# Two steps of a first chunk: exponents in a second PSUM bank and weight pieces taken in twos, in a Fourier-mixing and hard-swish kernel

## The chip, the cores and the metric

The kernel runs on one core of one Trainium2 chip. The metric is the time of one execution on the device in microseconds (us); lower is better.

## What is computed

The reference mixes a tensor with a two-dimensional Fourier transform, keeps the real part, and sends every row through a two-layer network with a hard-swish gate. `x` and the output are float32, the two weight matrices float64.

```python
x: (8, 3008, 256)      w_in: (256, 2048)      w_out: (2048, 256)
X = np.fft.fft(np.fft.fft(x, axis=1), axis=2).real      # (24064, 256) as rows
h = X @ w_in
g = h * np.clip(h + 3.0, 0.0, 6.0) / 6.0
out = g @ w_out                                         # (24064, 256)
```

## The kernel before

**The main work.** The eight batches are four pairs (`Pair`). The sequence transform of a pair is made in two stages (`stage1`, `stage2`); the transform along the 256 columns is folded into `w_in` (`fold_w_in`), so that its result lies in the SBUF tile `W1` (and one column of it in `WN`). A pair has 24 chunks, and a chunk eight steps, one for each two of the sixteen blocks of 128 hidden units. A step of a chunk is `mlp1` (four matmuls on TensorE into the PSUM tiles `u` and `v`, line 337, then two additions, two scaled relus on ScalarE, L379, and two gates on VectorE, L382, that leave the tile `a`), and `mlp2` (seven matmuls, L422, over seven combinations of blocks of `w_out`, kept in `G`). Only the first chunk of all uses the plain form `mlp2_first` (four matmuls of 512 columns, L406, "acc" below), since the combined blocks of `G` aren't ready. All matmuls on float32 show as two passes in the records, so four matmuls are "x8".

**The weights.** Both weight matrices come in as 64-bit words, in sixteen pieces of 128 x 512 (512 KB each), and are turned into float32 by hand, from the two 32-bit halves of each word. Pieces 0 to 3, 8, 9, 10 and 11 belong to `w_in`, the others to `w_out`. For a piece `j`:

- `exponent_a(j)`, here a(j): two ScalarE instructions (L532) that put exponent bytes into a tile `PM`, of which there are two, used in turn;
- `mantissa(j)`, here m(j): two VectorE instructions (L553, L554);
- `exponent_b(j)`, here ex(j): two fp16 matmuls on TensorE (L542) that gather the exponents in a PSUM tile; for pieces 5 and 15 it is one VectorE subtraction instead;
- `exponent_c(j)`, here c(j): one ScalarE instruction (L545) in place in PSUM;
- `join(j)`: VectorE multiplies mantissa and exponent into a tile `wi` (`w_in`, L562, one instruction) or into `G` (`w_out`, L568, two).

`head(j)` is a(j), m(j) and, for some pieces, the load of a later one (`load_w`, a DMA on GpSimd's queue, POOL). `tail(j)` is c(j) and the join. `unit(j)` is ex(j), then `head(j + 1)`, then `tail(j)`. When two pieces of `w_in` are joined, `fold_w_in(n, h)` multiplies them with the cosine table on TensorE (tile `spare`, L591; with h = 0 also the small matmuls `pw`, L599), and a postponed copy (`copy_all`) takes the product to `W1` and `WN` on ScalarE (L603, L605). With h = 1 the `WN` part goes out as four small DMAs on SyncE's queue, SP (L608).

**The order.** Nothing is scheduled by a planner (`manual_schedule`): every engine executes its instructions in the order in which the Python code emits them. In the first chunk the weights are converted between the steps. `DUE` says which units follow which step; `fourth_step` writes the fourth step's order out by hand. So the third step (s = 2) is `mlp1` of step 4 (here mlp1(3), counting from 0), acc(2), `unit(8)`, `unit(9)`; the fourth (s = 3) is acc(3), fold(1,0), units 10 and 11, ex(12), fold(3,0), ex(13), mlp1(4), fold(1,1), fold(3,1). SyncE's queue meanwhile holds, in this order, the late part of the stage-1 result (`zd<-z`, L833), stage-2 tables (`T`, L614), the four `WN` DMAs of this step, then more of `zd` and `T` and, in the sixth step, the load `g<-zd` (L268) that `stage2` needs in the eighth.

**PSUM.** There are eight banks: four of pool `ps_a`, three of `ps_h` (tag "uv": `u`, `v` and `pw` take them in turn) and one of `ps_d`. While `starting` holds, exponents go to `ps_h`; afterwards `bank` gives them the single bank of `ps_d`. So ex(j + 1) must wait there until join(j) has read the bank.

Of the kernel before, what the change touches and what calls it, by code (L numbers as in the profile page):

```python
# [7 lines left out]
F32 = mybir.dt.float32  # L8
I32 = mybir.dt.int32
U32 = mybir.dt.uint32  # L10
I16 = mybir.dt.int16
U8 = mybir.dt.uint8
F16 = mybir.dt.float16
# [45 lines left out]
def kernel(  # L59
# [11 lines left out]
    P = nc.NUM_PARTITIONS  # L71
# [29 lines left out]
    ps_h = ctx.enter_context(tc.tile_pool(name="ps_h", bufs=3, space=PSUM))  # L101
# [90 lines left out]
    starting = [True]  # L192

    def bank(shape, name):
        if starting[0]:
            return ps_a.tile(shape, F32, tag="acc", name=name)
        return ps_d.tile(shape, F32, tag="d", name=name)
# [129 lines left out]
    def mlp1(ch, fc):  # L327
        gr, of, nq = ch.ck // 2, ch.ck % 2 * TB, ch.nq
        q, qn = ch.pr.q[gr], ch.pr.qn[gr]
        u = ps_h.tile([P, 2, TB], F32, tag="uv", name="u")  # L330
        v = ps_h.tile([P, 2, TB], F32, tag="uv", name="v")
        for blk, ps in ((0, u), (1, v)):

            r = slice(0, P - blk)
            for i in range(2):
                f = fc + i * NF
                nc.tensor.matmul(ps[:, i, 0:nq], W1[r, blk, f * P:(f + 1) * P], q[r, blk, of:of + nq],  # L337
                                 start=True, stop=True)
        s = spool.tile([P, 2, TB], F32, tag="s", name="s")
        for i in range(2):  # L340
            f = fc + i * NF
            nc.vector.scalar_tensor_tensor(s[:, i, 0:nq], qn[:, of:of + nq], WN[:, f:f + 1], u[:, i, 0:nq],  # L342
                                           op0=AL.mult, op1=AL.add)


        a = apool.tile([P, 2, 2, TB], F32, tag="a", name="a")
        t = spool.tile([P, 2, 2, TB], F32, tag="t", name="t")
        ch.a[fc] = a
        if ch.last:
            activate_last(a, t, s, u, v, nq)  # L350
            return
        nc.vector.tensor_tensor(u[:], s[:], v[:], op=AL.add)  # L352
        relu(t[:, 0], u[:], 1.0 / 6.0)
        nc.vector.tensor_tensor(v[:], v[:], s[:], op=AL.subtract)  # L354
        relu(t[:, 1], v[:], -1.0 / 6.0)
        gate(a[:, 0], t[:, 0], u[:])
        rev, tk, vk = (m.rearrange("p i (k n) -> p (i k) n", n=N2) for m in (a[:, 1], t[:, 1], v[:]))
        gate(rev[:, :, ::-1], tk, vk)
# [19 lines left out]
    def relu(t, h, scale):  # L378
        nc.scalar.activation(t, h, AF.Relu, bias=half[:], scale=scale)  # L379

    def gate(dst, t, h):
        nc.vector.scalar_tensor_tensor(dst, t, 1.0, h, op0=AL.min, op1=AL.mult)  # L382
# [17 lines left out]
    def mlp2_first(ch, fc):  # L400
        a = ch.a.pop(fc)
        for h in range(2):
            if fc == 0:
                ch.acc[h] = ps_a.tile([P, 2, TB], F32, tag="acc", name="acc")
            for f in range(2):
                nc.tensor.matmul(ch.acc[h][:], G[:, (B11, B12, B21, B22)[2 * f + h], fc, :], a[:, :, f],  # L406
                                 start=(fc == 0 and f == 0), stop=(fc == NF - 1 and f == 1))
        if fc == NF - 1:
            ch.r = epool.tile([P, 2, 2, TB], F32, tag="r", name="r")
            for h in range(2):  # L410
                for m in range(2):
                    nc.scalar.mul(ch.r[:, m, h], ch.acc[h][:, m], (1 - 2 * m) / WS)
# [59 lines left out]
    def store(ch, m):  # L472
        o = epool.tile([P, TB // DH, 2, DH], F32, tag="o", name="o")
        for h in range(2):
            turn(ch, o, m, h)
        send(ch, o, m)
# [15 lines left out]
    wpool = wctx.__enter__()  # L492
# [4 lines left out]
    WB = 512  # L497
# [3 lines left out]
    raw, difs, exs, fracs, w = {}, {}, {}, {}, {}  # L501
# [26 lines left out]
    def exponent_a(j):  # L528
        top = raw[j][:].bitcast(I16).rearrange("p (n four) -> p n four", four=4)[:, :, 3]
        for i in range(2):  # L530
            low = PM[j % 2][:, i].bitcast(U8).rearrange("p (n two) -> p n two", two=2)[:, :, 0]
            nc.scalar.activation(low, top, AF.Identity, bias=bias[:, i:i + 1], scale=(1 - 2 * i) / 16.0)  # L532

    def exponent_b(j):
        pm = [PM[j % 2][:, i].bitcast(F16) for i in range(2)]
        if j in (5, len(PIECES) - 1):
            exs[j] = wpool.tile([P, WB], F32, tag="ex", bufs=2, name="ex")
            nc.vector.tensor_tensor(exs[j][:], pm[0], pm[1], op=AL.subtract)
            return
        exs[j] = ps_h.tile([P, WB], F32, tag="uv", name="ex") if starting[0] else bank([P, WB], "ex")  # L540
        for i in range(2):
            nc.tensor.matmul(exs[j][:], E[:, i], pm[i], start=(i == 0), stop=(i == 1))  # L542

    def exponent_c(j):
        nc.scalar.activation(exs[j][:].bitcast(I32), exs[j][:], AF.Identity, scale=2.0 ** 23)  # L545

    def mantissa(j):
        st = raw.pop(j)
        hi = st[:].rearrange("p (n two) -> p n two", two=2)[:, :, 1]
        lo = st[:].bitcast(U32).rearrange("p (n two) -> p n two", two=2)[:, :, 0]  # L550
        top = wpool.tile([P, WB], I32, tag="top", bufs=3, name="top")
        frac = top[:].bitcast(F32)
        nc.vector.tensor_scalar(top[:], hi, 0xFFFFF, 0x100000, op0=AL.bitwise_and, op1=AL.bitwise_or)  # L553
        nc.vector.scalar_tensor_tensor(frac, lo, 2.0 ** -32, top[:], op0=AL.mult, op1=AL.add)  # L554
        fracs[j] = frac
# [79 lines left out]
    nc.sync.dma_start(out=CE[:], in_=dim[:, :, D:])  # L635
    E = wpool.tile([P, 2, P], F16, tag="E", name="E")
    nc.scalar.copy(E[:], CE[:])
    PM = [wpool.tile([P, 2, WB], I16, tag="PM", bufs=2, name="PM") for j in range(2)]
    for pm in PM:
        nc.vector.memset(pm[:].rearrange("p i n -> p (i n)").bitcast(I32), 0x64006400)  # L640
    for b in range(2):
# [7 lines left out]

    def head(j):  # L650
        exponent_a(j)
        mantissa(j)
        if j in NEXT:
            load_w(NEXT[j])

    def tail(j):
        exponent_c(j)
        join(j)

    def unit(j):  # L660
        exponent_b(j)
        if j + 1 < len(PIECES):
            head(j + 1)
        tail(j)

    def fold_now(n, *hs):
        for h in hs:
            fold_w_in(n, h)

    def copy_all():  # L670
        while copies:
            copies.pop(0)()


    def see(x):
        nc.gpsimd.tensor_copy(seen[:], x)
# [28 lines left out]

    head(0)
    exponent_b(0)
    keep_awake(1)
    head(1)
# [71 lines left out]
    def chunk(s):  # L781
        p, ck, fc = steps[s]
        return chunks[p][ck], fc


    DUE = [(6,), (7,), (8, 9), (), (14,), (15,), (), ()]
    head(4)
    mlp1(*chunk(0))
    exponent_b(4)
# [5 lines left out]
    unit(5)  # L795


    def fourth_step():
        mlp2_first(*chunk(3))
        fold_now(1, 0)  # L800
        unit(10)
        copy_all()
        unit(11)
        exponent_b(12)
        fold_now(NWI // 2 + 1, 0)
        head(13)
        tail(12)
        copy_all()
        exponent_b(13)
        tail(13)  # L810
        mlp1(*chunk(4))
        fold_now(1, 1)
        fold_now(NWI // 2 + 1, 1)
        head(14)
        copy_all()

    prev = None
    for s, (p, ck, fc) in enumerate(steps):
        if ck == 0 and fc == 0:
            at = beside(p)  # L820
        for f, a in at.get(ck * NF + fc, ()):
            f(*a)
        if s < NF:

            if s == 3:
                fourth_step()
            else:
                mlp1(*chunk(s + 1))
                if s == NF - 1:
                    combine(*chunk(NF))  # L830
                mlp2_first(*chunk(s))
            for dst, src in later[2 * s:2 * s + 2]:
                nc.sync.dma_start(out=dst, in_=src)  # L833
            for j in DUE[s]:
                unit(j)

            if s == 5:
                see(chunk(s + 1)[0].a[s + 1][:, 0, 0, 0:1])
                mix_w_out(0)
                mix_w_out(1)  # L840
            if s == NF - 1:
                mlp1(*chunk(NF + 1))
        else:
            if s + AHEAD < len(steps):
                mlp1(*chunk(s + AHEAD))
            if s + 1 < len(steps):
                combine(*chunk(s + 1))
            if s < NF + 2:
                mix_w_out(s - NF + 2)
            if prev and fc < 3:  # L850
                if fc > 0:
                    store(prev, fc - 1)
                elif not prev.first:
                    finish(prev)
            mlp2(*chunk(s))
        if fc == NF - 1:
            prev = chunks[p][ck]
# [81 lines left out]
```

## Time and profile before

| | |
|---|---|
| median of 3 runs | 1976.12 us (1975.09 to 1976.62) |
| span of the profiled execution | 1975.1 us |
| TensorE busy, share of the span | 99% |
| VectorE, GpSimd, ScalarE busy | 73%, 71%, 35% |
| chain that ended last | TensorE 93%, VectorE 3%, others 1% or less |
| TensorE clock in fortieths of the span | full, but for 0.9 in the first and 0.8 in the second |

One fortieth of the span is 49.4 us, so the second one covers 49.4 to 98.8 us, where the first chunk's steps lie. A line of the timeline holds start, duration, engine, source line, operation, tiles, and in brackets how long the engine was idle before it and who ended that. A line of the chain holds start, duration, engine and tile. [...]two exponent matmuls show 0.59 us and the next instruction can start 0.43 us after them.

### The profile page before, as it was taken

The page shows a single profiled execution, that of the slowest core. Times are in us where ns is not written, and L with a number is a line of the kernel's source. Part 1 is how long each engine was busy: PE and PEld are TensorE (multiplying, and loading weights), DVE is VectorE, ACT ScalarE, POOL GpSimd, SP SyncE. Part 2 cuts the span into 40 slices and gives each one's busy share as a digit, 9 for nine tenths or more (in the row PEclk, how much of TensorE's full clock was granted, in tenths as well). Part 3 has the DMA queues.
Part 4 walks back from the last instruction along what each step waited for, and adds up shares of the span by engine and source line. Part 5 has one row for each costly group of instructions (what it writes and reads, how often), then busy time and mean ns, then how long its engine had stood idle before and what let it go on. Part 6 is the DMA issues. An engine that isn't in the chain of part 4 may idle for free.

```text
span 1975.1 us, 27615 instructions
## 1 busy us (share of the span) xinstructions
PE 1945.8 (99%) x9134; PEld 1674.1 (85%) x9134; DVE 1437.4 (73%) x2776; ACT 686.9 (35%) x1167; POOL 1399.9 (71%) x1593
## 2 busy tenths in 40 slices
PE   8899999999999999999999999999999999999998
PEld 4578888888998888888898888888889888888887
DVE  6687767677787676776777777777678777777776
ACT  5533333333333333333333333333333333333332
POOL 3068778786787787777668877778667667666765
PEclk9899999999999999999999999999999999999999
DMA  8421121211112121220111221212110101111000
GB/s 229 159 68 52 51 57 50 54 48 35 27 36 51 41 51 52 56 52 24 38 31 30 66 58 43 51 41 55 36 25 21 29 16 23 27 23 27 18 21 20
DMA packets 144701, 93.34 MB, mean 47 GB/s; under 512 B 116743, under 2 KB 130059, under 8 KB 144558
## 3 DMA queue, kind: packets, MB, share of 16 engines
q1 hardware_dynamic: 134294, 57.89, 12.0%
q0 software_dynamic: 9472, 33.49, 6.0%
q8 instruction: 72, 1.18, 0.3%
q14 instruction: 71, 0.58, 0.1%
q10 hardware_dynamic: 792, 0.20, 0.0%
HBM read 54.22 MB, written 37.32 MB: 46 GB/s over the span
## 4 chain that ended last, share of the span: by engine, by line
PE 93%; DVE 3%; ACT 1%; DMA 1%; issue 1%; SPq 0%; DVEq 0%; POOL 0%; ACTq 0%
PE acc L422 55%; PE v L337 16%; PE u L337 16%; PE ps L213 2%; PE ps L286 2%; DVE a L382 1%; PE acc L406 1%; DMA xt<-in_x_dram,IX 1%; DVE s L342 1%; ACT t L379 1%; PE spare L591 0%; DVE o L480 0%; DVE u L363 0%; ACT PM L532 0%; DMA T<-in_c_stage_dram 0%
## 5 line engine op out<-in xcount | busy, mean ns | idle before, releaser
L396 POOL TENSOR_TENSOR c<-a 128x512 f32<-128x512 f32 (+1 forms) x375 | 468.8, 1250 | 398.9 <-PE acc L422 353.6
L422 PE MATMUL acc<-c,G 128*128 128x256 f32 (+1 forms) x3008 | 696.9, 374 | 0.0
L379 ACT ACTIVATE t<-u,half 128x512 f32<-128x512 f32 (+1 forms) x384 | 260.7, 679 | 1102.6 <-DVE u L352 1023.1
L422 PEld LDWEIGHTS acc<-c,G 128*128 128x128 f32 x3008 | 565.4, 190 | 71.1
L342 DVE SCALAR_TENSOR_TENSOR s<-qn,WN,u 128x256 f32<-128x256 f32 (+1 forms) x768 | 330.1, 471 | 352.2 <-PE u L337 351.6
L422 PE MATMUL acc<-a,G 128*128 128x256 f32 (+1 forms) x2256 | 538.8, 374 | 0.0
L422 PEld LDWEIGHTS acc<-a,G 128*128 128x128 f32 x2256 | 423.4, 190 | 54.9
L337 PE MATMUL v<-q,W 127*128 127x256 f32 (+1 forms) x1536 | 389.4, 375 | 2.3 <-DVE a L382 2.3
L337 PE MATMUL u<-q,W 128*128 128x256 f32 (+1 forms) x1536 | 388.8, 375 | 0.0
L382 DVE SCALAR_TENSOR_TENSOR a<-t,u 128x512 f32<-128x512 f32 (+2 forms) x448 | 263.8, 600 | 102.7 <-ACT t L379 99.1
L337 PEld LDWEIGHTS u<-q,W 128*128 128x128 f32 x1536 | 286.5, 190 | 56.6 <-issue 15.8
L337 PEld LDWEIGHTS v<-q,W 127*128 127x128 f32 x1536 | 288.6, 190 | 42.5 <-DVE a L382 1.9
L396 POOL TENSOR_TENSOR c<-a,c 128x256 f32<-128x256 f32 (+1 forms) x375 | 268.9, 717 | 29.4
L396 POOL TENSOR_TENSOR c<-c,a 128x256 f32<-128x256 f32 (+1 forms) x375 | 268.6, 716 | 29.4
L352 DVE TENSOR_TENSOR u<-s,v 128x512 f32<-128x512 f32 x352 | 245.0, 696 | 38.3 <-DVE s L342 1.8
L382 DVE SCALAR_TENSOR_TENSOR a<-t,v 128x512 f32<-128x512 f32 (+1 forms) x480 | 263.4, 565 | 0.3 <-ACT t L379 0.2
L379 ACT ACTIVATE t<-v,half 128x512 f32<-128x512 f32 (+1 forms) x384 | 260.6, 679 | 0.4 <-issue 0.2
L354 DVE TENSOR_TENSOR v<-v,s 128x512 f32<-128x512 f32 x352 | 243.7, 692 | 0.0
L396 POOL TENSOR_TENSOR r<-w,e 128x256 f32<-128x256 f32 (+1 forms) x92 | 88.8, 987 | 3.6
L430 ACT ACTIVATE e<-acc 128x512 f32<-128x512 f32 (+2 forms) x186 | 84.5, 545 | 3.4 <-PE acc L422 3.3
L480 DVE STREAM_TRANSPOSE o<-r 128x256 f32<-128x256 f32 (+1 forms) x192 | 72.5, 415 | 0.2
L213 PE MATMUL ps<-y,F 94*96 94x512 f32 x120 | 61.3, 601 | 5.2 <-ACT q L289 5.2
(97 smaller groups left out, 798.0 us busy)
## 6 DMA issues: line engine op xcount, KB each, us to landing
out_dram<-o SPq DMA_DIRECT2D x746, 32.0 KB
zd<-z SPq DMA_DIRECT2D x24, 384.0 KB
g<-zd SPq DMA_DIRECT2D x36, 256.0 KB
xt<-in_x_dram POOLq DMA_DIRECT2D x21, 384.0 KB, 4.3
qn<-qd SPq DMA_DIRECT2D x19, 256.0 KB
st<-in_moe_w_in_dram POOLq DMA_DIRECT2D x8, 512.0 KB, 8.3
st<-in_moe_w_out_dram POOLq DMA_DIRECT2D x8, 512.0 KB, 5.7
g<-zd SPq DMA_DIRECT2D x12, 257.0 KB
```

The lines of the kernel that those rows point to most:

```text
L213: nc.tensor.matmul(ps[0:PZ], F[0:PR, 0:PZ], y[:, 2 * i:2 * i + 2, :], start=True, stop=True)
L286: nc.tensor.matmul(ps[:, blk, u * P:n].rearrange("p (b k) -> p b k", b=2), g[:, kk, blk * (P + 1):blk * (P + 1) + P], T[:, :, gr, blk, kk, ...
L337: nc.tensor.matmul(ps[:, i, 0:nq], W1[r, blk, f * P:(f + 1) * P], q[r, blk, of:of + nq], start=True, stop=True)
L342: nc.vector.scalar_tensor_tensor(s[:, i, 0:nq], qn[:, of:of + nq], WN[:, f:f + 1], u[:, i, 0:nq], op0=AL.mult, op1=AL.add)
L352: nc.vector.tensor_tensor(u[:], s[:], v[:], op=AL.add)
L354: nc.vector.tensor_tensor(v[:], v[:], s[:], op=AL.subtract)
L379: nc.scalar.activation(t, h, AF.Relu, bias=half[:], scale=scale)
L382: nc.vector.scalar_tensor_tensor(dst, t, 1.0, h, op0=AL.min, op1=AL.mult)
L396: (eng or nc.gpsimd).tensor_tensor(out, in0, in1, op=AL.add)
L422: nc.tensor.matmul(ch.acc[i // 2][:, i % 2, 0:ch.n], G[:, i, fc, :], mv, start=(fc == 0 and i % 2 == 0), stop=(fc == NF - 1), skip_group_c ...
L430: nc.scalar.mul(ch.e[:, k:i + 1, 0:ch.n], ch.acc[i // 2][:, 0:i + 1 - k, 0:ch.n], 1.0 / WS)
L480: nc.vector.transpose(o[:, 0:n // DH, h], ch.r[:, m, h, 0:n].rearrange("p (j i) -> p j i", i=DH))
```

## The change

The order on TensorE, ScalarE and VectorE in the third and fourth steps of the first chunk is changed, and two buffers with it:

- `PM` has three tiles in place of two (one more memset at the start), and piece j uses tile j mod 3.
- Exponents 8, 10 and 12 go into a bank of `ps_h`; 9, 11 and 13 stay in the bank of `ps_d`.
- A new `third_step`: a(9) stands ahead of mlp1(3), ex(8) ahead of acc(2), and join(8) ahead of m(9). Piece 10's head moves from here to the fourth step.
- The fourth step takes pieces 10 and 11, then 12 and 13, in twos: both heads, both exponents, the fold, both tails.

```diff
     def exponent_a(j):
...
-            low = PM[j % 2][:, i].bitcast(U8).rearrange("p (n two) -> p n two", two=2)[:, :, 0]
+            low = PM[j % len(PM)][:, i].bitcast(U8).rearrange("p (n two) -> p n two", two=2)[:, :, 0]
...
-        exs[j] = ps_h.tile([P, WB], F32, tag="uv", name="ex") if starting[0] else bank([P, WB], "ex")
+
+        h = starting[0] or (j % 2 == 0 and 8 <= j < 14)
+        exs[j] = ps_h.tile([P, WB], F32, tag="uv", name="ex") if h else bank([P, WB], "ex")
...
-    PM = [wpool.tile([P, 2, WB], I16, tag="PM", bufs=2, name="PM") for j in range(2)]
+    PM = [wpool.tile([P, 2, WB], I16, tag="PM", bufs=3, name="PM") for j in range(3)]
...
     def head(j):
         exponent_a(j)
+        head_b(j)
+
+    def head_b(j):
         mantissa(j)
...
-    DUE = [(6,), (7,), (8, 9), (), (14,), (15,), (), ()]
+    DUE = [(6,), (7,), (), (), (14,), (15,), (), ()]
...
+    def third_step():
+        exponent_a(9)
+        mlp1(*chunk(3))
+        exponent_b(8)
+        mlp2_first(*chunk(2))
+        tail(8)
+        head_b(9)
+        exponent_b(9)
+        tail(9)
+
     def fourth_step():
         mlp2_first(*chunk(3))
+        head(10)
+        head(11)
+        exponent_b(10)
+        exponent_b(11)
         fold_now(1, 0)
-        unit(10)
+        tail(10)
+        tail(11)
+        head(12)
+        head(13)
         copy_all()
-        unit(11)
         exponent_b(12)
+        exponent_b(13)
         fold_now(NWI // 2 + 1, 0)
-        head(13)
         tail(12)
+        tail(13)
         copy_all()
-        exponent_b(13)
-        tail(13)
         mlp1(*chunk(4))
...
-            if s == 3:
-                fourth_step()
+            if s in (2, 3):
+                (third_step if s == 2 else fourth_step)()
```

More of the change, by code (lines that the diff above doesn't have):

```diff
@@ L530, in exponent_a @@
         for i in range(2):
-            low = PM[j % 2][:, i].bitcast(U8).rearrange("p (n two) -> p n two", two=2)[:, :, 0]
+            low = PM[j % len(PM)][:, i].bitcast(U8).rearrange("p (n two) -> p n two", two=2)[:, :, 0]
             nc.scalar.activation(low, top, AF.Identity, bias=bias[:, i:i + 1], scale=(1 - 2 * i) / 16.0)
     def exponent_b(j):
-        pm = [PM[j % 2][:, i].bitcast(F16) for i in range(2)]
+        pm = [PM[j % len(PM)][:, i].bitcast(F16) for i in range(2)]
         if j in (5, len(PIECES) - 1):
```

## The prediction, made before the changed kernel ran

> **What bounds the kernel now.** I read the page first: TensorE (PE) is busy for 99% of the span, and the chain that ended last is PE for 93%. From about 128 us on, the chain in order of time is nothing but PE work joined end to end. So an edit in the first chunk gains what PE loses there, if what follows moves up as a block. PE's waits between 60 and 130 us have three rows; the first is the one that the change aims at:
>
> ```profile
> PE ex L542 <- DVE wi L562: 5.6, 3, 2.4
> PE v L337 <- DVE a L382: 1.5, 1, 1.5
> PE acc L406 <- DVE G L568: 0.9, 1, 0.9
> ```
>
> Three times an exponent matmul waits until VectorE (DVE) has joined the piece before it, 5.6 us in all: ex(j + 1) needs the one bank that join(j) reads. The chain shows what comes after:
>
> ```profile
> 77.03 0.59 PE ex L542 x2
> 77.62 3.43 PE acc L406 x8
> 81.05 1.73 PE spare L591 x8
> 82.78 0.79 PE pw L599 x8
> ...
> 87.77 1.01 PE ex L542 x2
> 88.78 3.41 PE spare L591 x8
> 92.20 1.50 PE pw L599 x8
> 93.69 0.88 PE ex L542 x2
> 94.57 1.71 PE u L337 x4
> 96.28 1.16 PE v L337 x4
> 97.43 3.46 PE spare L591 x16
> ```
>
> The same eight `spare` passes take 1.73 us at 81 us and 3.41 at 88.8; sixteen take 3.46 at 97.4. Everything from 87.8 to about 96.7 is at half speed. The table by stretches says why (the third figure from the right is the granted clock):
>
> ```profile
> 81.00:84.00 3.00, 3.00 (x19) 2.41 (x18) 0.00 (x0) 0.00 (x0) 0.00 (x0) 1.00 0.00 0
> 84.00:87.00 3.00, 0.61 (x3) 0.19 (x2) 1.72 (x3) 2.94 (x7) 0.00 (x0) 0.92 0.00 0
> 87.00:90.00 3.00, 2.23 (x6) 1.59 (x6) 2.28 (x5) 1.90 (x3) 0.00 (x0) 0.50 0.00 0
> 90.00:93.00 3.00, 3.00 (x12) 2.55 (x10) 0.19 (x1) 0.59 (x1) 0.00 (x0) 0.50 0.00 0
> 96.00:99.00 3.00, 3.00 (x14) 2.55 (x13) 2.27 (x6) 0.80 (x2) 0.00 (x0) 0.88 0.00 0
> ```
>
> PE works 0.61 us between 84 and 87; the granted clock then falls to 0.50 and is whole again near 96.7. Slices of 0.4 us put the fall at 86.5: 10.2 us at half clock. The loss is thus two things, waits and the clock that they cost.
>
> [...]here no gap lasted over 1.9 us. [...]83.1 to 86.5 us held 1.5 us of PE work, 44%[...]. [...]acc(3) had its `a` by 75.2 (gate at 74.51 plus 0.69) and began at 77.46, behind ex(9).[...]
>
> **The loss before, as a sum.** mlp1(3) leaves PE at about 70.55 and the two last folds start at 97.43 in the chain: 26.9 us. The work between, by full-clock rows: two acc 2 x 3.44 (eight passes of 0.43), six exponents 6 x 0.43, two `spare` 2 x 1.73, two `pw` 2 x 0.79, mlp1(4) 1.72 = 16.2. Lost 10.7. Of it idle: ex(8) ends issuing at 74.42, ex(9) starts 77.03 (2.6); 83.99 to 85.41 (1.4); 85.84 to 87.77 (1.9): 5.9. Half clock, by the chain lines against their full-clock twins: 0.42 + 1.68 + 0.71 + 0.44 + 0.85 + 0.30 = 4.4. Together 10.3; the rest is rounding of overlaps.
>
> **The new order, step by step.** Durations as in the trace; ScalarE (ACT) instructions of a(j) come 0.66 apart, c(j) takes 0.58, DVE multiplies 0.69 and follow each other after 0.61, m(j) 1.07.
>
> *Third step.* a(9) moves ahead of the relus: ACT is free from 70.7 (after c(7)) to 73.13, so its 1.4 us fit in. ex(8) moves ahead of acc(2). Its new wait is on DVE, for the gate that frees an old `v` bank, at 69.63; a(8) ends at 70.24. PE comes there at 70.55: no wait, and acc(2) behind it runs 70.97 to 74.41. ex(9) finds its bank free (join(7) ended about 71.5) and PM(9) full: 74.41. acc(3) then waits for the gate of mlp1(3), ending 75.20: about 0.4 idle, from 74.84 to 75.25. Before, it started at 77.46. DVE joins 8 at 75.16 (c(8) on ACT 74.48 to 75.06), m(9), joins 9 until 77.5.
>
> *Fourth step.* acc(3) until 78.7. a(10), a(11) on ACT 75.6 to 78.3, under acc(3). ex(10), ex(11) at 78.7 and 79.14, fold(1,0) 79.57 to 82.1; joins 8 and 9 are done. Under the fold ACT does c(10), c(11) from 79.34, a(12), a(13) to 83.1; DVE joins 10 and 11 by 81.2. ex(12) at 82.1; ex(13) waits 0.4 for a(13) until 83.14. fold(3,0) waits for `spare`, which the copy frees at 83.66: 0.3. It and `pw` run 83.7 to 86.2. Behind it u waits for the `W1` copy, 85.6 to 86.2: nothing. mlp1(4) leaves PE at 87.95, where before it was 97.43: 9.5 us sooner. The new waits are 0.4 + 0.4 + 0.3 = 1.1 against the 5.9 + 4.4 that go[...].
>
> *Other edits.* The third memset is 0.485 us of DVE at 3.8 us, hidden in its 4.37 us wait for `x`. No matmul is added. On POOL the load of piece 15 is issued about 0.5 us later than 76.80, behind m(9); POOL then had nothing for 33.6 us, and piece 15 is used past 111 us. Loads 12 to 14 are not moved; the DMA engines are all but idle from 75.4 to 78, so those pieces had landed, and a(12) at 80.4 doesn't wait. On SP the order is the same; it stood 30.7 us on the `W1` copies at 101.36, which now end near 92.5, 0.3 us later against PE than before; `zd`, `T` and `g` behind them move up with it. `stage2` had no wait at 117.0 and the DMA engines had gone quiet at about 114.
>
> *After the steps.* mlp1(5) starts where the two folds end, 91.4; a of mlp1(4) is ready at 91.0, acc(4) wants it at 93.1. The unlike terms are small, so the lead of 9.4 us (9.5, less 0.1 for the later copies) passes into the stretch that is PE end to end.
>
> Bounds of what no row shows. The wait of ex(13) and of fold(3,0) hangs on ACT's queue: 0.2 us to 1.6 us for both. A weight load after a wait can add up to 0.3 each, three times.[...] None of these waits can be a gain: each adds time or nothing, and the fixed work excludes more than 10.7 in all. So the gain is 8.2 to 10.7, and I take 9.4. The span of 1975.1 stands beside runs of 1975.09 to 1976.62: I subtract from their median, 1976.12 - 9.4 = 1966.7.
>
> **Rivals.**
>
> *The clock falls all the same*, in the new gaps at 82 to 84 us or at a later one (1.54 us at 125.8).[...] Price 10.2 us at half speed, 4.4 to 5.1: 1971.5.
>
> *Given back at `stage2`, slower.* If `g` and the tables were bound by the transfers and not by SP's wait, they would land where they land now, about 114, and PE would wait for them from 117.0 - 9.4 = 107.6: 6.4 us. [...]the half clock (5.1) follows: 11.5 against 9.4 gained, 1978.2. From a wait of about 4.3 us on it is no gain any more; from 8.3 us on slower by over 0.2% (1980.1). Against: the DMA engines move nothing between 81 and 103 us.
>
> *The change does less than it says*: the second bank is waited for too, or an ACT wait takes the whole place of the DVE wait; the clock stays whole yet half of the idle returns: 9.4 - 3 = 6.4, 1969.7.
>
> **Chances.** Main case 0.84, with 1964.9 to 1968.6 as its own range (the gain's bounds, and 0.5 us for the spread of runs). Less than it says 0.05, clock 0.06, given back 0.05, of which 0.02 within 0.2% and 0.03 beyond it. 0.2% of 1976.12 is 3.95 us, about what a measurement can tell from none; the limit is 1972.2, so a bad instance of the clock case counts as no change, 0.01. Faster 0.94, same 0.03, slower 0.03. The range 1964.4 to 1970.2 takes in the main case and the third rival.
>
> **What would show it.** Right: PE's waits lose the row "ex <- wi"; the granted clock is 1.00 from 84 to 99 us; `spare` with eight passes takes about 1.73 both times; acc(3) starts near 75.2; mlp1(4) ends near 88; the first L422 starts about 9.4 us before 128.3. Wrong: a new wait of over a microsecond on ACT PM or ACT W, a clock below 1.00 after 60 us, or a wait for DMA at `stage2`.

## The result and the profile after

| | before | after |
|---|---|---|
| median | 1976.37 us (6 runs, 1975.09 to 1978.09) | 1967.29 us (6 runs, 1966.91 to 1968.04) |
| span of the profiled execution | 1975.1 us | 1965.4 us |

The ratio is 0.9954, with a 95% interval of 0.9941 to 0.9967. The predicted time was 1966.7 us; 9.1 us were gained where 9.4 were foretold.

TensorE's waits between 60 and 130 us, in the profile after:

```profile
PE v L337 <- DVE a L382: 1.5, 1, 1.5
PE acc L406 <- DVE a L382: 0.3, 1, 0.3
PE ex L544 <- ACT PM L532: 0.2, 1, 0.2
```

The row "ex <- wi" with its 5.6 us is gone; two small rows stand in its place. (The row "acc <- G" of before is no gain: that wait ends at 59.16 us here and at 60.12 us there, so it only slips out of the window. Line numbers are shifted by 2 from the fold on.) The chain of work, in order of time (start, duration, what):

```profile
74.31 3.70 PE acc L406 x8
78.01 0.86 PE ex L544 x4
78.87 1.73 PE spare L593 x8
...
81.38 0.68 PE ex L544 x3
82.07 0.03 issue
82.10 0.56 ACT W L605
82.66 0.06 ACT WN L607
82.72 1.98 PE spare L593 x8
...
87.32 3.46 PE spare L593 x16
```

From 74 to 95 us the chain no longer leaves PE for joins; it leaves it once, for 0.65 us, for ScalarE's copies, where fold(3,0) waits for its bank. Its eight passes then take 1.98 us, and not 3.41. The clock in the same stretches:

```profile
81.00:84.00 3.00, 2.72 (x14) 1.70 (x14) 2.25 (x6) 2.67 (x6) 0.00 (x0) 1.00 0.00 0
84.00:87.00 3.00, 3.00 (x20) 2.74 (x19) 1.14 (x4) 0.75 (x2) 0.00 (x0) 1.00 0.00 0
87.00:90.00 3.00, 3.00 (x16) 2.64 (x15) 2.74 (x5) 1.80 (x3) 0.00 (x0) 1.00 0.00 0
```

The third figure from the right is 1.00 throughout, and PE works 2.72 to 3.00 us of each 3. (The clock row in the table of before needs a correction: a digit 9 there stands for 0.9 or more. The mean clock of before is 1.00 over the first 49.4 us and 0.90 over the second.)

**A ledger of the two profiles.** I cut the span at three points: the first u of mlp1(3), the two last folds (`spare` x16 in the chain), and the first L422 with 14 passes.

| stretch, us | before | after | gain |
|---|---|---|---|
| start to first u of mlp1(3) | 68.82 | 67.86 | 0.96 |
| from there to the two last folds | 28.61 | 19.46 | 9.15 |
| from there to the first L422 | 31.06 | 31.07 | -0.01 |
| from there to the end | 1846.6 | 1847.0 | -0.4 |

Only the second row holds reordered instructions. The first moves by itself from run to run: VectorE waits there for the gathers of `x` (6.9 us in six waits in this profile; 9.6 in that of the experiment with two PM tiles, which reaches mlp1(3) at 72.53), and behind such a wait, of 3.25 us, the clock fell in the experiment with two PM tiles. The third row says that the lead passes as a block. So the second row, measured inside one profile, is the sharp instrument, and I use it for the experiments ("the stretch" below); the medians stand beside it.

A profile is one execution, though, and says nothing of the others. For those there is the mean granted clock of a whole execution, which is recorded for every run of the experiments. In the thirteen profiles it is 0.998 or 0.999 where the clock stood at 1.00 from 69 to 120 us, 0.997 where it was at half for 3.4 or 6.8 us, and 0.996 where it was for 10.2 us. The six runs of the changed kernel have 0.998 or 0.999; 39 runs of the kernel before, made beside the experiments, have 0.994 to 0.997. So, by this measure, all of these runs of before had the half clock and none of the changed kernel did. The mean does not say where in the program it was.

### The profile page after: what moved, and what is told of

Its sections match the earlier page's. It is cut to its first block, busy times and chain, and to the rows that moved or that the text cites. A ratio compares the mean times of both kernels' runs of the same rounds, so it can differ in the third digit from the quotient of the medians.

```text
span 1965.4 us, 27617 instructions
## 1 busy us (share of the span) xinstructions
PE 1942.5 (99%) x9134; PEld 1671.3 (85%) x9134; DVE 1437.9 (73%) x2777; ACT 687.9 (35%) x1167; POOL 1399.7 (71%) x1593
## 4 chain that ended last, share of the span: by engine, by line
PE 93%; DVE 3%; DMA 1%; ACT 1%; issue 1%; SPq 0%; DVEq 0%; POOL 0%; ACTq 0%; POOLq 0%
PE acc L422 55%; PE v L337 16%; PE u L337 16%; PE ps L213 2%; PE ps L286 2%; DMA xt<-in_x_dram,IX 1%; DVE a L382 1%; PE acc L406 1%; DVE s L342 1%; ACT t L379 1%; PE spare L593 0%; DVE o L480 0%; DVE u L363 0%; ACT PM L532 0%; DMA T<-in_c_stage_dram 0%
## 5 line engine op out<-in xcount | busy, mean ns | idle before, releaser
L422 PE MATMUL acc<-c,G 128*128 128x256 f32 (+1 forms) x3008 | 696.9, 374 | 0.0
L422 PEld LDWEIGHTS acc<-c,G 128*128 128x128 f32 x3008 | 565.4, 190 | 71.1
L422 PE MATMUL acc<-a,G 128*128 128x256 f32 (+1 forms) x2256 | 538.8, 374 | 0.0
L422 PEld LDWEIGHTS acc<-a,G 128*128 128x128 f32 x2256 | 423.3, 190 | 55.0
L480 DVE STREAM_TRANSPOSE o<-r 128x256 f32<-128x256 f32 (+1 forms) x192 | 72.5, 415 | 0.2
```

Source lines behind the costliest of these rows:

```text
L422: nc.tensor.matmul(ch.acc[i // 2][:, i % 2, 0:ch.n], G[:, i, fc, :], mv, start=(fc == 0 and i % 2 == 0), stop=(fc == NF - 1), skip_group_c ...
L480: nc.vector.transpose(o[:, 0:n // DH, h], ch.r[:, m, h, 0:n].rearrange("p (j i) -> p j i", i=DH))
```

## Experiments

Theory A is that of the prediction: two losses, the idle time and the half clock that follows from it. The rivals stand in the expectations. Each expectation was written before its run.

**A filler in the gaps: no wait is taken away.** In the kernel before:

```diff
         copy_all()
+        filler = C[:].rearrange("p h d -> p (h d)")
+        keep_awake(1, filler)
         unit(11)
+        keep_awake(2, filler)
         exponent_b(12)
```

> The kernel before with three idle matmuls (128x512 float32 on the cosine table, result unused) in the gaps ahead of ex(11) and ex(12); no wait is taken away. Theory A (two losses: 5.9 us idle behind the one bank, and 4.4 us because that idle lowers the clock): the waits stay, the clock is 1.00 from 84 to 99 us, and the time falls by about 4.4 to 1972.0; the eight spare passes of fold(3,0) take 1.73 us. Theory B (the half clock isn't caused by the gaps, all of the gain is wait): clock falls as before, 1976.4.

Measured: 1971.68 us, ratio 0.9979 (0.9968 to 0.999); the stretch is 24.25 us, 4.36 less than before. Table by stretches and chain of this run:

```profile
84.00:87.00 3.00, 2.47 (x8) 1.04 (x7) 1.72 (x3) 2.90 (x7) 0.00 (x0) 1.00 0.00 0
87.00:90.00 3.00, 2.93 (x13) 1.92 (x12) 2.47 (x5) 1.98 (x4) 0.00 (x0) 1.00 0.00 0
```

```profile
87.83 0.59 PE ex L542 x2
88.42 1.73 PE spare L591 x8
```

ex(12) starts at 87.83, as late as before (87.77), but PE works through the gap and the clock stays at 1.00; `spare` takes 1.73. Work that computes nothing gains 4.4 us. Theory A holds, B falls: the half clock is caused by the gaps, and it is nearly half of the gain. (The gap ahead of ex(9) was left open. Seven of the nine runs have a mean clock of 0.998 or 0.999; the other two, 1974.96 and 1977.56 us, have 0.997 and 0.996, so the clock still fell in them.)

**The second bank alone.** In the kernel before:

```diff
-        exs[j] = ps_h.tile([P, WB], F32, tag="uv", name="ex") if starting[0] else bank([P, WB], "ex")
+        h = starting[0] or (j % 2 == 0 and 8 <= j < 14)
+        exs[j] = ps_h.tile([P, WB], F32, tag="uv", name="ex") if h else bank([P, WB], "ex")
```

> The kernel before with only the second bank: exponents 8, 10, 12 in ps_h, order and PM as before. Theory A: the waits for joins go, but in the old order ex(12) waits for a(12) on ScalarE and fold(3,0) for join(11) behind it, 3.2 us idle[...], so the clock falls all the same; only 1.9 us are gained, 1974.5. Theory C (the bank is the change, the order adds little): the waits and the clock loss both go, 1967 to 1970.

Measured: 1971.14 us, ratio 0.9973 (0.9962 to 0.9983); the stretch is 23.15, a gain of 5.5. TensorE's waits and the clock of this run:

```profile
PE ex L543 <- ACT PM L532: 2.6, 4, 1.5
```

```profile
81.00:84.00 3.00, 1.54 (x9) 0.71 (x9) 1.50 (x3) 2.15 (x5) 0.00 (x0) 1.00 0.00 0
84.00:87.00 3.00, 2.72 (x7) 1.76 (x6) 2.28 (x6) 2.62 (x5) 0.00 (x0) 0.57 0.00 0
87.00:90.00 3.00, 3.00 (x18) 2.55 (x17) 0.41 (x2) 1.23 (x3) 0.00 (x0) 0.86 0.00 0
```

The joins are no longer waited for; ScalarE is, as A said, and the clock falls, as A said. But my number was 3.4 us too pessimistic: the clock is low for 3.4 us here (slices of 0.4 us: 84.45 to 87.86), not 10.2, and costs 1.6 us (`spare` 3.34 against 1.73). Neither A's figure nor C's "both losses go" is right: the bank turns a wait for VectorE into a shorter one for ScalarE, and the order is needed for the rest, 3.7 us.

**Each step alone.** First the new third step, with the old fourth (head(10) stands ahead of its fold); then the old third step with the second bank and the new fourth. Both are edits of the changed kernel:

```diff
-        h = starting[0] or (j % 2 == 0 and 8 <= j < 14)
+        h = starting[0] or j == 8
...
         mlp2_first(*chunk(3))
         head(10)
-        head(11)
-        exponent_b(10)
-        exponent_b(11)
         fold_now(1, 0)
+        unit(10)
...
```

> The new third step alone (exponent 8 in ps_h, 9 in ps_d), the fourth step as before, with head(10) ahead of its fold. Theory A: acc(3) starts near 75.2 us on the scale of before, 2.2 us sooner; ex(11) and ex(12) wait 1.5 and 2.2 us as before and the clock still falls, so 2.2 us are gained, 1974.2. If the clock should not fall, 6.6 us, 1969.8.

```diff
-    DUE = [(6,), (7,), (), (), (14,), (15,), (), ()]
+    DUE = [(6,), (7,), (8, 9), (), (14,), (15,), (), ()]
...
-        head(10)
         head(11)
...
-            if s in (2, 3):
-                (third_step if s == 2 else fourth_step)()
+            if s == 3:
+                fourth_step()
```

> The third step as before (units 8 and 9, head(10) with them) but with exponents 8, 10, 12 in ps_h, and the new fourth step. Theory A: ex(9) waits 1.2 us for a(9) on ScalarE, the fourth step has only 0.7 us of waits and the clock stays at 1.00: 8.7 us gained, 1967.7 to 1968.0, some 0.7 above the changed kernel. If the third step carried half of the gain, 1971 to 1972.

TensorE's waits in the two runs, the third step alone first:

```profile
PE ex L544 <- DVE wi L564: 3.2, 2, 1.8
```

```profile
PE ex L544 <- ACT PM L532: 1.1, 3, 0.6
```

Measured: the third step alone 1972.35 us, ratio 0.9975 (0.9966 to 0.9983), stretch 23.81 (4.8 gained); the fourth alone 1967.88 us, ratio 0.9959 (0.9945 to 0.9973), stretch 20.13 (8.5 gained). With the third step alone PE still waits 3.2 us for two joins and the clock falls, though for 3.4 us only (85.7 to 89.2): acc(3) is 2.2 us sooner, as foretold, and the other 2.6 us are a shorter half clock. With the fourth alone, the table by stretches has 1.00 everywhere, and 1.1 us of waits for ScalarE are left. The mean clock agrees: 0.996 or 0.997 in all twelve runs of the third step alone, 0.998 or 0.999 in all five of the fourth. The two gains add up to more than 9.15: the half clock was shorter with the one and gone with the other, and it can be saved only once. The fourth carries nearly all; the third adds 0.7 to it. But the run of the fourth alone has exponent 8 in the second bank too, and so a part of the third step's gain: acc(3) starts 7.2 us after the first u of mlp1(3) in it, against 8.6 before and 6.5 in the changed kernel.

**The third PM tile.** In the changed kernel:

```diff
-    PM = [wpool.tile([P, 2, WB], I16, tag="PM", bufs=3, name="PM") for j in range(3)]
+    PM = [wpool.tile([P, 2, WB], I16, tag="PM", bufs=2, name="PM") for j in range(2)]
```

> The changed kernel with two PM tiles again (piece j uses tile j mod 2). Theory A: the third tile buys nothing in this order: a(10), a(11), a(12), a(13) would overwrite what ex(8), ex(9), ex(10), ex(11) read, and those end before ScalarE comes to them (a(11) at 76 us after ex(9) at 74, a(13) at 80.8 after ex(11) at 79). Same time within 0.2 us, 1967.3. Rival: the third tile is what lets the heads run in twos; then ScalarE waits for ex(11) and 0.5 to 1.5 us come back.

Measured: 1967.71 us, ratio to before 0.9949 (0.9937 to 0.9962); the stretch is 19.44 against 19.46. The tile buys nothing in this order. The profiled run of this kernel took 1971.28 us and still has the short stretch: it came to mlp1(3) 4.7 us later than the changed kernel. TensorE's timeline shows why:

```profile
20.41 0.25 PE L220 MATMUL pt<-y,F 94*96 94x4 f32 x2
...
25.07 1.02 PE L622 MATMUL awake<-Z,ones 128*128 128x512 f32 x2
29.34 0.36 PE L220 MATMUL pt<-y,F 94*96 94x4 f32 x2 [3.25 <-DVE y L178]
29.56 3.71 PE L213 MATMUL ps<-y,F 94*96 94x512 f32 x4
33.06 1.91 PE L622 MATMUL awake<-Z,ones 128*128 128x512 f32 x2
...
37.40 1.02 PE L622 MATMUL awake<-Z,ones 128*128 128x512 f32 x2
...
38.37 1.94 PE L213 MATMUL ps<-y,F 94*96 94x512 f32 x4
```

Behind a wait of 3.25 us the same four passes take 3.71 us and not 1.94. The same instructions, `pt` to the second `awake` behind it, take 8.06 us from 29.34 and 4.66 from 20.41; the 3.4 us between them make some 6.8 us at half clock, an estimate from these rows; the `pt` at 29.34 is already slow, with 0.36 us. So the start of the program varies with the gathers and with the clock that waiting for them costs.

**How much idle brings the clock down.** In the changed kernel, n = 2 and n = 5 ScalarE copies that compute nothing:

```diff
         head(12)
+        for _ in range(n):
+            nc.scalar.copy(spare[1][:], C[:])
         head(13)
```

> The changed kernel with two idle ScalarE copies (128x512, the cosine table into a free PSUM tile) ahead of a(13), so that TensorE waits some 1.2 us longer at ex(13) and fold(3,0), about 1.6 us in all[...]. Theory A[...]: no fall of the clock, +1.2 us, 1968.5. Theory D (any new gap here lowers the clock): +3 or more.

> The same with five copies, some 3.1 us more, 3.5 us idle in all. Theory A: the clock falls to 0.50 for one window of 3.4 us, in which the dense passes of fold(3,0) run at half speed, 1.7 us on top of the wait: +4.8, 1972.1 (if it stays low for three windows, +8). If idle cost only itself: +3.1, 1970.4.

Measured: with two, 1969.86 us, ratio to before 0.9964 (0.9951 to 0.9977), stretch 20.59, which is 1.13 more than after, and a clock of 1.00 at 81 to 84 us, where PE works only 1.75 of 3:

```profile
81.00:84.00 3.00, 1.75 (x7) 1.00 (x7) 1.12 (x3) 2.98 (x7) 0.00 (x0) 1.00 0.00 0
```

With five, 1971.39 us, ratio 0.9971 (0.9959 to 0.9983), stretch 24.05, 4.6 more than after. The table of this second run:

```profile
84.00:87.00 3.00, 0.59 (x2) 0.10 (x1) 0.06 (x1) 2.94 (x6) 0.00 (x0) 1.00 0.00 0
87.00:90.00 3.00, 2.91 (x8) 2.21 (x8) 1.41 (x4) 1.23 (x4) 0.00 (x0) 0.52 0.00 0
90.00:93.00 3.00, 3.00 (x18) 2.73 (x17) 0.34 (x1) 0.75 (x2) 0.00 (x0) 0.91 0.00 0
```

In these two executions the short gap costs itself; the long one costs itself (3.0 us) and the clock for one step of 3.4 us (a window, in the expectations), `spare` at 3.59 us in place of 1.98. In the stretch both were foretold within 0.2 us. But the profiled run with two copies is the fastest of its five, with a mean clock of 0.998, like the next (1967.44 and 1967.77 us); the other three have 0.997 and take 1969.86 to 1970.95. The clock fell somewhere in them, and by the medians the short gap costs 2.6 us and not the 1.2 foretold. So rival D is refuted for one execution only: in others this gap may well bring the fall, which no profile here shows. With five copies all six runs have 0.997.

**What ends the half clock.** In the kernel with five copies, and in the kernel before, `pw` stands ahead of `spare` in fold(3,0):

```diff
+        if (n, h) != (NWI // 2 + 1, 0):
+            products()
         fs = range(cs.start // P, cs.stop // P)
...
+        if (n, h) == (NWI // 2 + 1, 0):
+            products()
```

(`products` holds the four matmuls into `spare`.) The kernel before was profiled once more, too. E and F are guesses that these runs test: with `pw` first the half clock lasts longer (E), or as long as before (F).

> The kernel of the five idle copies (3.5 us idle, one window at 0.50 then) with one thing more: in fold(3,0) the four one-column matmuls pw stand ahead of the four dense ones of spare. Theory E[...]: the first 1.6 us after the fall are then pw, the clock stays at 0.50 for two windows or more, 6.8 us in place of 3.4, and the stretch from mlp1(3) to the two last folds grows by 1.7 us or more, beside 0.6 for u, which now waits for the copy of spare. Theory F[...]: one window again, 3.4 us.

> The kernel before once more, unchanged, for a second profile: whether the half clock lasts 10.2 us in it again. Theory A: a fall to 0.50 near 86 us on the scale of the first profile; its length a whole number of windows of 3.4 us[...]; the time goes with it by 1.7 us for each.

> The kernel before with pw ahead of spare in fold(3,0), as in the run with the five idle copies. Theory E: in the first profile of before the window from 89.9 to 93.3 held 1.3 us of pw; with dense passes there the clock is back one window sooner, 6.8 us at 0.50 in place of 10.2, and 1.7 us are gained, less 0.2 to 0.4 for u's wait. Theory F: 10.2 us as before.

Measured, one run each: 1971.15, 1975.85 and 1974.97 us, beside 1974.38 for the kernel before. With five copies and `pw` first the clock is low for one step only (85.2 to 88.6) and the stretch is 24.26, 0.2 more than with `spare` first: Theory E's number is missed. Its chain shows that the run is a weak test, though:

```profile
84.86 1.06 PE pw L605 x8
85.92 3.25 PE spare L594 x8
```

The fall came at 85.2, when `pw` had begun, so only 0.7 us of `pw` lie in the 3.4 us behind it, not the 1.6 that E reckoned with. In the kernel before with `pw` first it is low for two (86.2 to 93.0) and the stretch is 27.25, 1.4 less, which E foretold, but one profile can't part that from a fall that comes elsewhere, as the second profile of the kernel before shows:

```profile
75.00:78.00 3.00, 1.81 (x4) 0.96 (x4) 2.66 (x5) 2.88 (x5) 0.71 (x1) 0.77 0.21 25
78.00:81.00 3.00, 3.00 (x6) 1.17 (x5) 1.20 (x3) 0.78 (x2) 0.00 (x0) 0.66 0.39 150
...
84.00:87.00 3.00, 1.47 (x8) 0.67 (x8) 1.44 (x3) 2.09 (x5) 0.00 (x0) 0.97 0.00 0
87.00:90.00 3.00, 1.36 (x4) 0.89 (x4) 2.00 (x4) 2.49 (x5) 0.00 (x0) 0.50 0.00 0
90.00:93.00 3.00, 3.00 (x10) 2.35 (x8) 0.75 (x2) 0.27 (x1) 0.00 (x0) 0.50 0.00 0
93.00:96.00 3.00, 3.00 (x18) 2.67 (x17) 0.65 (x2) 1.33 (x3) 0.00 (x0) 0.89 0.00 0
```

The same program, and the clock falls twice: at 76.6 for 3.4 us, behind the first gap of 2.4 us, and near 87 for 6.8. acc(3) takes 5.08 us in its chain, against 3.43 in the first profile. The stretch is 28.39 against 28.61: the half clock lasts 10.2 us in all both times, cut otherwise. What is shown: it lasts 3.4 us (five falls in the stretch), 6.8 (two) or 10.2 (one), so it comes in whole steps of 3.4, and which gap brings it changes from execution to execution. Where nothing but dense matmuls follows the fall (bank alone, third step alone, five copies, and the first fall here) it ended after one step; where PE waits another 1.0 to 1.8 us after it (both profiles of before, and before with `pw` first) it lasted two or three. Waiting does not account for all of it: at the start of the run with two PM tiles PE was busy from 29.34 to 33.06 us, with passes of 94 x 96 (`pt` and `ps` above), so for all of a first step by the estimate there, and a second step followed. Dense 128 x 128 matmuls fit better. Counted from the chains, each step in the stretch that ended the half clock held 2.7 us of them or more, and each that did not 2.3 us or less; in the first profile's second step that was 2.3 us of `spare`, beside 1.1 us of `pw`. So Theory E is neither borne out nor refuted, and why the first profile had a third step stays open.

**More of the same?** The wait of fold(3,0) for its bank, and the 1.5 us row "v <- a" that both kernels have in the ninth step, where the third mlp1 in a row (counting from mlp1(8)) finds its `v` bank taken, are the targets:

```diff
-        copy_all()
         exponent_b(12)
         exponent_b(13)
         fold_now(NWI // 2 + 1, 0)
+        copies.pop(0)()
...
-            if s + AHEAD < len(steps):
+            if s + AHEAD < len(steps) and s > NF:
                 mlp1(*chunk(s + AHEAD))
...
             mlp2(*chunk(s))
+            if s == NF:
+                mlp1(*chunk(s + AHEAD))
```

> The changed kernel with two of the waits left taken away: fold(3,0) goes into the other spare bank, so that it doesn't wait for the copy of fold(1,0) (0.3 us), and in the ninth step mlp1(10) stands behind the first seven-product step, whose operands are ready, in place of ahead of it (TensorE waits 1.5 us there for a bank). Theory A: 0.3 + 1.0 to 1.5 us less, 1965.5 to 1966.0. Rival: the wait moves to the next step's v bank, 0.3 or less is left, 1967.0.

Measured: 1967.47 us, ratio to before 0.9955 (0.9943 to 0.9967): no difference from the changed kernel that these runs can tell. The chain in the ninth and tenth steps:

```profile
114.34 3.02 PE acc L422 x14
117.36 0.88 PE u L337 x4
...
121.57 1.13 PE v L337 x4
122.70 3.02 PE acc L422 x14
```

The stretch is 19.08, 0.38 less than after: the first edit did what was foretold. The second only moved its wait: L422 runs in the old gap, and the `v` behind it waits 1.6 us for a bank one step later. The rival holds for it.

## Why the prediction was right

**The loss before.** Waits 5.9 and half clock 4.4 us were foretold from the chain. The filler run parts them: 4.36 us came back with every wait still in place. The remaining 4.79 of the 9.15 is the net of the waits.

**The third step.** acc(3) was to start 4.7 us after mlp1(3) had left PE (70.55 to 75.25), behind a 0.4 us wait for the gate. Measured: PE leaves mlp1(3) at about 69.59 and starts acc(3) at 74.31, 4.7 us later, with a wait row of 0.3. ex(8) had no wait, and a(9) ran in the gap ahead of the relus (ScalarE 69.70 to 71.1, the relu at 72.18).

**The fourth step.** The three new waits were put at 1.1 us; counted in the same way (from where the matmul ahead lets the next one start) they are about 1.0: 0.4 ahead of acc(3), 0.35 at ex(13), 0.25 at fold(3,0). No fall of the clock was foretold, and none came. The stretch gained 9.15 us where 9.5 was worked out. The fixed work of 16.2 us, with 1.7 for mlp1(3), and 1.0 of waits give 18.9 of the 19.46: some 0.5 us of small seams, such as u taking 0.97 in place of 0.86 us, were not in my sum. That is the term that was mis-sized. (The 0.3 us that the prediction allows for a weight load behind a wait is an estimate; the rows fit it: `v` takes 1.13 us at 117.25, behind its wait of 1.5 us, and 0.86 at 122.27, without one.)

**After the steps.** The lead was to pass whole into the PE-bound stretch: 31.06 and 31.07 us. SyncE's longest wait for ScalarE's copies shrank from 30.7 to 21.6 us, and `zd`, `T` and `g` moved up behind it; no wait for a DMA came at `stage2`. The rival "given back at `stage2`" is excluded by that row. Behind it the prediction read the chain of before as nothing but PE work. It is not quite: about 58 us of it past 128 us lie off PE, for instance from 1012 to 1023 us. The lead could have been lost there; the ledger's last row, with 0.4 us, says that it was not.

**Other edits at nothing.** The third memset makes DVE's 1.02 us into 1.57, ahead of a 3.75 us wait for `x`. It costs nothing, and by the experiment the tile gains nothing. Piece 15 is first read at 104.74 us in the profile before, by a(15), and not past 111 as the prediction has it; its load was issued at 76.80, so the half microsecond did not matter.

**What was not right in the reasoning.** The prediction read "10.2 us at half clock" as a property of the kernel before, and the fall as the price of the gaps ahead of ex(11) and ex(12). The clock stood at 1.00 around the 2.45 us gap of that profile:

```profile
75.00:78.00 3.00, 0.97 (x4) 0.58 (x4) 2.90 (x6) 2.94 (x6) 0.71 (x1) 1.00 0.06 23
```

The second profile of the same program has a fall behind that very gap, with 0.77 in the same stretch. Neither reading was wrong for the profile it came from. The total was the same in both profiles, but it is no constant of the kernel: the mean clock of the other runs of before ranges from 0.994 to 0.997. Nor does the share of work in some 3.4 us sort these cases. In before with `pw` first PE worked 42% of the time from 72.5 to 76.0 us and acc(3) behind it ran at full clock (3.43 us), while in the second profile it worked 59% from 83.4 to 86.8 us (0.8 us of it `pw`) and the clock fell. Taking one profile for the kernel also made the expectation for the bank alone 3.4 us too high.

## What to carry to other kernels

A wait on TensorE can be worth more than its length: here 5.9 us of waits cost 10.3. In these runs that happened where PE worked for 59% of some 3.4 us or less, in some executions and not in others. Test that by filling the gap with idle matmuls; if the time falls (here by 4.36 us in the stretch), the clock was part of the price, and closing only some of the gaps may bring the whole of that part back. A second PSUM bank takes away only the wait for the bank: if the next operand's producer stands late in its own engine's order, that is what is waited for next (2.6 us for ScalarE with the bank alone). Compare stretches inside a profile, from one instruction to another, when the start of the program varies by more than the effect, and set the mean clock of every run beside the one that was profiled.

## What the runs showed of the hardware that was not expected

- The half clock came in whole steps of 3.4 us, one, two or three of them, in different places in two executions of one program.
- It came without 3.4 us of idle: PE had worked about 1.5 of the 3.4 us ahead of the fall in the first profile. A gap that left 1.75 us of work in 3 us did not bring it in the one execution that was profiled.
- The busy time of PE alone sorted neither the falls nor their ends: a fall came after 59% of work and not after 42%, and 3.7 us in which PE was busy throughout, with passes of 94 x 96, did not end the half clock.
- The start of the program, up to the first mlp1(3), took between 67.02 and 72.53 us in these profiles, with the same instructions but for one memset. The latest holds a wait of 3.25 us behind a gather of `x` and, by the estimate above, some 6.8 us at half clock after it.
